# Transposes of the attention probabilities as two 64-row tiles, in turn with the scores by head

## Chip, cores, metric

The kernel runs on one core of one Trainium2 chip. The metric is the device time of one execution in microseconds (us). TensorE (PE) multiplies matrices into PSUM, VectorE (DVE) and ScalarE (ACT) read PSUM and SBUF, GpSimd (POOL) works in SBUF, and SyncE (SP) issues most of the DMA.

## The reference, cut to what matters

Attention with a bias that a small network makes of the relative positions, and behind it a gated feed-forward network (FFN) with a convolution over the sequence. There are 4 batches, 8 heads, 576 positions and 64 elements a head; all is float32.

```python
scores = scale * np.matmul(q, k.transpose(0, 1, 3, 2))      # (4, 8, 576, 576)
scores = scores + bias.transpose(2, 0, 1)[None, :, :, :]
scores = scores - np.max(scores, axis=-1, keepdims=True)
attn = np.exp(scores)
attn = attn / (np.sum(attn, axis=-1, keepdims=True) + 1e-09)
out = np.matmul(attn, v)
...
h = np.maximum(x @ w_in, 0.0)       # x: (4, 576, 512), w_in: (512, 1024)
...
return (h * gate @ w_out)
```

## The kernel before

The work has three stages: the bias (up to about 66 us, with the first units of attention between its steps), the attention loop (to about 316 us) and the FFN.

The attention loop goes over 16 passes `n` in `seq`, a pass being one pair of heads and one batch. A pass has five units `t` in the order 1, 2, 3, 4, 0 (`units`, line 85), and `ui` is a unit's place in that order. A unit of t = 1 to 4 is 128 query rows of both heads; the unit of t = 0 is the first 64 rows of both heads on top of each other, so it counts as one head (`heads`, line 544).

For each unit and head there are three steps. `scores` (line 327) multiplies q and k in two tiles of TensorE, 64 rows by 128 columns each, into two banks of a `psS` tile (two buffers); VectorE adds the bias and takes the row's minimum of the negative (line 348). `expo` (line 359) is one exponential on ScalarE, with the row's sum collected in `sms`. `transposes` (line 375) turns the probabilities, so that their keys lie on the partitions: four 128x128 blocks for each head on TensorE (line 388, as float32r against an identity), into one bank of `psT` (three buffers), which ScalarE copies to `pt` for head 0 and VectorE for head 1 (line 393). The last 64 keys of both heads are one further block (line 400) in a further bank, copied by VectorE (line 403). A small marker on ScalarE (line 323, `turned_sp`) precedes the transposes of head 0.

`pv_parts` (line 411) then multiplies v and `pt` in column tiles of 128 by 64. Its parts are kept in `fill` and are issued by `pv_share` after the transposes of the units at `ui` 0, 2 and 4. For most passes 20 instructions cover 256 or, for t = 0, 64 query columns. ScalarE copies the product out to `x` (lines 444 and 446).

The sums of a pass are inverted in the next one: `invert(n - 1)` on VectorE (lines 452 and 453), behind the unit at `ui` 1; a transpose of them by TensorE with the transposes of the unit at `ui` 2 (line 402), copied by VectorE (line 406); through DRAM by SyncE's DMA queue (`normalise`, line 461); and a multiplication on GpSimd (`apply_norm`, line 474), issued at `ui` 4.

The order of each engine's instructions is the order of the program. In the loop (line 604) an iteration `u` issues the scores of unit u + 2 and the exponentials of unit u + 1, head by head, then the transposes of unit u, head by head, each followed by one step of a weight job (`job_steps`: one step with ScalarE's line 96 and VectorE's line 97, then VectorE's lines 99 and 103, then GpSimd's lines 130 and 131), then `invert`, the products and the rest:

```python
for h in range(2):
    ...            # scores(*flat[u + 2], h); expo(*flat[u + 1], h)
for h in range(2):
    if h in heads(t):
        transposes(n, t, h, n - 1 if h and ui == 2 and n else None)
    next(job_steps, None)
```

Of the kernel before, what the change touches and what calls it, by code (L numbers as in the profile page):

```python
# [9 lines left out]
F32 = mybir.dt.float32  # L10
F32R = mybir.dt.float32r
# [8 lines left out]
def attention_ffn_kernel(  # L20
# [11 lines left out]
    nc = tc.nc  # L32
# [6 lines left out]
    P = 128  # L39
    TL = S % P  # L40
    NT = S // P
    NM = NT * P
# [23 lines left out]
    psT = pool(ctx, "psT", 3, space=PSUM)  # L66
# [8 lines left out]
    ident = const.tile([P, P], F32, name="ident")  # L75
    identr = const.tile([P, P], F32R, name="identr")
# [13 lines left out]
    def dve(o, i):  # L90
        nc.vector.tensor_copy(o, i)  # L91
# [41 lines left out]
    with tc.manual_schedule():  # L133
# [163 lines left out]
        r_p = pool(att, "r", 2)  # L297
        rb_p = pool(att, "rb", 1)

        rr_t = [vz_p.tile([P, P], F32, name=f"rr{i}") for i in range(2)]  # L300
        for r in rr_t:
            nc.gpsimd.memset(r, 0.0)
        rts = {}
# [71 lines left out]
        def transposes(n, t, h, sums=None):  # L375
            g = group(n, t)
            if (n, g) not in ptt:
                ptt[n, g] = pt_p.tile([P, 9, 2 * P], F32, name="pt") if g else pt0s[n % 2]
            pt = ptt[n, g]
            c0 = P if t == 2 or t == 4 and n else 0  # L380
            cs = slice(c0, c0 + P)
            if h == 0:
                turned_sp(n, t)
            spf = spt[n, t][0]
            ps = psT.tile([P, 512], F32, name="tp")
            for c in range(4):
                j = 5 * h + c
                tr = nc.tensor.transpose(  # L388
                    ps[:, c * P:(c + 1) * P].bitcast(F32R), spf[:, j * P:(j + 1) * P], identr
                )  # L390
                if c == 0:
                    tc.add_manual_dep(tr.ins, exps.pop((n, t, h)).ins.name, DATA)
            (dve if h else act)(pt[:, 5 * h:5 * h + 4, cs], ps.rearrange("p (c x) -> p c x", c=4))
            if h or not t:
                ps = psT.tile([P, 512], F32, name="tp")


                rows = P if t else TL
                cols = P if n else rows
                nc.tensor.transpose(ps[0:cols, 0:P].bitcast(F32R), spf[:, NM:NM + cols], identr)  # L400
                if sums is not None:
                    nc.tensor.transpose(ps[:, P:2 * P], rr_t[sums % 2], ident)
                dve(pt[0:rows, 4, cs], ps[0:rows, 0:P])
                if sums is not None:
                    rts[sums] = r_p.tile([9, P], F32, name="rt")
                    dve(rts[sums], ps[0:9, P:2 * P])

        ops_t = {}
        waiting = {}
# [1 line left out]
        def pv_parts(n, g):  # L411
            p, b = seq[n]
# [3 lines left out]
            def part(c):  # L416
# [7 lines left out]
                for h in range(2):  # L424
                    hs = slice(D * h, D * h + D)
                    if g:
                        slot = (0 if h else 5) if c == 4 else 6 + c if h else 1 + c
                        rhs = pt[:, 4 if c == 4 else 5 * h + c, 0:width]
                    else:
                        slot = 10 + c if h else 1 + c  # L430
                        rhs = pt[:, c, TL * h:TL * h + TL]
                    nc.tensor.matmul(  # L432
                        po[hs, oc], vt[:, slot, :], rhs, start=(c == 0), stop=(c == 4)
                    )
# [169 lines left out]
        for u, (n, t) in enumerate(flat):  # L604
            p, b = seq[n]
            ui = units.index(t)
            for h in range(2):
# [2 lines left out]
                        scores(*flat[u + 2], h)  # L610
                if u + 1 < NU and h in heads(flat[u + 1][1]):
                    expo(*flat[u + 1], h)
            for h in range(2):
                if h in heads(t):
                    transposes(n, t, h, n - 1 if h and ui == 2 and n else None)
                next(job_steps, None)
# [25 lines left out]
            if u + 2 < NU:  # L642
                n2, t2 = flat[u + 2]
                p2, b2 = seq[n2]
                if b2 == B - 1 and p2 + 1 < NP:
                    load_bias(p2 + 1, t2)
            if ui == 1 and n > 0:
                invert(n - 1)

            parts = len(fill) if u < 4 else pv_share[ui]  # L650
# [217 lines left out]
```

## Time and profile before

| | |
|---|---|
| median of 3 runs | 533.89 us (531.12 to 534.03) |
| profiled execution, its own time | 534.86 us |
| its span in the trace | 533.1 us |
| PE, DVE, ACT, POOL busy | 505.7, 385.4, 303.5, 103.9 us |

Busy time is the time covered by an engine's instructions in the record. PEld is the loading of weights into TensorE, which can lie under its matmuls. The end of a matmul is modelled and comes after its last column was streamed, so the distance between the starts of two matmuls tells the cost of the first, and a block's duration is longer than its share of the engine. A float32 multiplication of `scores` or `pv_parts` shows as two instructions.

### The profile page before, as it was taken

To read this page: it belongs to the slowest core of one execution; us is meant where nothing else is said; L and a number is where in the kernel's file an instruction comes from. 1 tells how busy PE (TensorE), PEld (TensorE's weight loads), DVE (VectorE), ACT (ScalarE), POOL (GpSimd) and SP (SyncE) were. 2 spreads that over 40 slices of the span, in tenths; PEclk is the share of its full clock that TensorE was granted. 3 is DMA by queue.
4 is the path that set the end of the run, shared out by engine and by line. 5 is a ranking of instruction groups with operands and counts; after the bars stand their busy time and mean duration, and the time that the engine had idled before them with its cause. 6 is when DMAs were issued, how large, how long until landed. Compare 5 with 4: busy or idle time off the path is not lost.

```text
span 533.1 us, 10413 instructions
## 1 busy us (share of the span) xinstructions
PE 505.7 (95%) x3871; PEld 376.4 (71%) x3871; DVE 385.4 (72%) x888; ACT 303.5 (57%) x733; POOL 103.9 (19%) x123
## 2 busy tenths in 40 slices
PE   5988999999999999999989999799999999999995
PEld 3332466676666666666656678788998899899984
DVE  6989685676778778788776854994699169928910
ACT  5888785677666777666775654652362135215510
POOL 1000000112222222212222521571016002500000
PEclk9999999999899999999998999989999999999998
DMA  6689654697556975579753121000100200020011
GB/s 158 251 242 354 220 136 109 152 292 181 153 140 157 299 185 155 139 177 289 190 138 86 60 80 46 0 2 6 73 1 0 81 20 1 1 79 2 1 39 59
DMA packets 32700, 63.40 MB, mean 119 GB/s; under 512 B 5490, under 2 KB 11146, under 8 KB 32650
## 3 DMA queue, kind: packets, MB, share of 16 engines
q1 hardware_dynamic: 32506, 62.66, 40.4%
q8 instruction: 30, 0.49, 0.4%
q14 instruction: 20, 0.16, 0.1%
q10 hardware_dynamic: 144, 0.08, 0.1%
HBM read 46.74 MB, written 15.98 MB: 118 GB/s over the span
## 4 chain that ended last, share of the span: by engine, by line
PE 59%; DMA 10%; DVE 8%; POOL 3%; issue 3%; ACT 2%; SPq 1%; POOLq 0%; DVEq 0%
PE s L495 17%; PE tp L719 14%; PE o L432 10%; PE s L341 8%; PE tp L388 5%; PE o L719 4%; DMA r_d<-rt 3%; DMA rb<-r_d 3%; DVE sp L348 2%; POOL x L474 2%; DMA qk<-in_qk_dram 1%; DMA vt<-in_v_dram 1%; DVE cv L694 1%; DVE pt L91 1%; ACT sp L362 1%
## 5 line engine op out<-in xcount | busy, mean ns | idle before, releaser
L348 DVE CUSTOM_DVE_ANT_0 sp<-s,bt 128x576 f32<-128x576 f32 x144 | 103.4, 750 | 52.2 <-PE s L341 35.8
L362 ACT ACTIVATE sp<-sp,nm 128x576 f32<-128x576 f32 x144 | 110.2, 769 | 8.9 <-DVE nm L348 8.9
L495 PE MATMUL s<-xs,wi 128*128 128x288 f32 x768 | 106.4, 301 | 2.9 <-ACT h L507 2.9
L495 PEld LDWEIGHTS s<-xs,wi 128*128 128x128 f32 x768 | 105.4, 193 | 3.4 <-ACT h L507 3.1
L341 PE MATMUL s<-qk 64*128 64x288 f32 x640 | 100.7, 431 | 2.2 <-DVE nm L348 1.9
L432 PE MATMUL o<-pt,vt 128*64 128x256 f32 (+2 forms) x940 | 89.8, 338 | 0.7 <-ACT x L88 0.7
L388 PEld LDWEIGHTS tp<-identr,sr 128*128 128x128 f32 x576 | 53.9, 140 | 34.8 <-issue 20.8
L341 PEld LDWEIGHTS s<-qk 64*128 64x128 f32 x640 | 54.7, 186 | 30.7 <-issue 7.1
L432 PEld LDWEIGHTS o<-pt,vt 128*64 128x64 f32 x940 | 53.9, 139 | 24.4 <-issue 2.2
L88 ACT ACTIVATE pt<-tp 128x512 f32<-128x512 f32 x80 | 46.9, 586 | 41.4 <-PE tp L388 41.4
L719 PE MATMUL tp<-wo,g 128*128 128x512 f32 x288 | 70.1, 389 | 0.0
L388 PE MATMUL tp<-identr,sr 128*128 128x128 f32 x576 | 66.2, 254 | 2.8 <-DVE pt L91 2.8
L91 DVE COPY pt<-tp 128x512 f32<-128x512 f32 (+2 forms) x144 | 60.8, 458 | 6.0 <-PE tp L400 3.1
L694 DVE SCALAR_TENSOR_TENSOR cv<-h,cw,cv 128x575 f32<-128x575 f32 x64 | 60.4, 944 | 2.4 <-ACT cv L689 0.4
L719 PEld LDWEIGHTS tp<-wo,g 128*128 128x128 f32 x288 | 54.0, 188 | 11.0
L474 POOL TENSOR_TENSOR x<-x,rb 128x576 f32<-128x576 f32 x16 | 23.3, 1453 | 177.4 <-ACT sr L323 90.6
L260 PE MATMUL s<-y,pars 128*32 128x512 f32 (+8 forms) x352 | 45.9, 502 | 5.0 <-ACT st L286 2.2
L243 DVE TENSOR_SCALAR y<-tl,inv,nb 128x512 f32<-128x512 f32 (+8 forms) x116 | 49.8, 504 | 0.0
L507 ACT ACTIVATE h<-s 128x576 f32<-128x576 f32 x32 | 20.8, 651 | 47.2 <-PE s L495 47.1
L700 ACT ACTIVATE cv<-cv 128x576 f32<-128x576 f32 x32 | 21.8, 682 | 29.7 <-DVE cv L694 29.7
L260 PEld LDWEIGHTS s<-y,pars 128*32 128x32 f32 x352 | 15.2, 113 | 29.3 <-DVE y L243 13.2
L130 POOL TENSOR_SCALAR xs<-x 128x576 fp32r<-128x576 f32 x16 | 15.1, 945 | 83.5 <-PE s L495 83.5
(68 smaller groups left out, 486.6 us busy)
## 6 DMA issues: line engine op xcount, KB each, us to landing
qk<-in_qk_dram SPq DMA_DIRECT2D x32, 320.0 KB
bt<-bias_d SPq DMA_DIRECT2D x32, 288.0 KB
bias_d<-st SPq DMA_DIRECT2D x14, 607.0 KB
qk<-in_qk_dram SPq DMA_DIRECT2D x32, 144.0 KB
rb<-r_d SPq DMA_DIRECT2D x32, 144.0 KB
out_dram<-o SPq DMA_DIRECT2D x17, 256.0 KB
raw_w<-in_moe_w_in_dram SPq DMA_DIRECT2D x16, 256.0 KB
vt<-in_v_dram SPq DMA_DIRECT2D x16, 224.0 KB
```

What stands on the lines that cost most here:

```text
L88: nc.scalar.activation(o, i, AF.Copy)
L91: nc.vector.tensor_copy(o, i)
L243: nc.vector.tensor_scalar(y, dist[:, 0:n], inv[:, ig:ig + 1], nb1, op0=ALU.mult, op1=ALU.max)
L260: nc.tensor.matmul(ps[32 * j:32 * j + 32, a // 512 if n > 512 else blk % 2, 0:min(n - a, 512)], w2b, ys[j][:, a:min(n, a + 512)], start=Tr ...
L341: nc.tensor.matmul(ps[:, a, 0:HS], qt[rows, qo:qo + P], qt[rows, KO + hh * HS:KO + hh * HS + HS], start=(i == 0), stop=(i == len(ops) - 1),)
L348: nc.vector.tensor_tensor_reduce(out=halves(spt[n, t][0][:, h]), in0=ps[:, :, 0:HS], in1=halves(bt[:, h]), op0=ALU.add, op1=ALU.min, scale ...
L362: exps[n, t, h] = nc.scalar.activation(sp[:, h], sp[:, h], AF.Exp, bias=nm[:, h:h + 1], scale=-1.0, accum_out=sms[n][:, col:col + 1],)
L388: tr = nc.tensor.transpose(ps[:, c * P:(c + 1) * P].bitcast(F32R), spf[:, j * P:(j + 1) * P], identr)
L432: nc.tensor.matmul(po[hs, oc], vt[:, slot, :], rhs, start=(c == 0), stop=(c == 4))
L495: nc.tensor.matmul(ps[:, a, 0:HS], wi[c][:, pw, cs], xss[b, c][:, px, a * HS:(a + 1) * HS], start=(i == 0), stop=(i == 3 * KC - 1),)
L694: nc.vector.scalar_tensor_tensor(out=cv[:, o:o + S - 1], in0=h[:, i:i + S - 1], scalar=cw[:, f, kk:kk + 1], in1=cv[:, o:o + S - 1], op0=AL ...
L719: nc.tensor.matmul(ps, lhs(f, gi), wo[f][:, wj, cs], start=(f == 0 and i == 0), stop=(f == FC - 1 and i == 2),)
```

## The change

Each transpose of 128 rows becomes two of 64 rows in the two row tiles that the scores use. The results of the two row halves go to two banks, `ps[0]` and `ps[1]`, so every call of `transposes` takes two `psT` tiles, where head 0 took one and head 1 two. The last block goes into the same banks, after the four blocks for t = 0 and ahead of them in the order of issue for head 1. ScalarE copies the first half and VectorE the second, for both heads: 256 columns each, or 320 with the last block; for t = 0 with its 64 rows the last block is a copy of its own. `pt` is laid out anew (blocks 0 to 3 head 0, 4 to 7 head 1, 8 the last). The transpose of the inverted sums becomes two of 64 rows, with two copies.

In the loop the two passes over the heads become one: scores, exponential and transposes of head 0, then those of head 1. `invert(n - 1)` moves from the unit at `ui` 1 to that at `ui` 0, from n = 2 on.

```diff
@@ transposes
-            ps = psT.tile([P, 512], F32, name="tp")
-            for c in range(4):
-                j = 5 * h + c
-                tr = nc.tensor.transpose(
-                    ps[:, c * P:(c + 1) * P].bitcast(F32R), spf[:, j * P:(j + 1) * P], identr
-                )
...
-            (dve if h else act)(pt[:, 5 * h:5 * h + 4, cs], ps.rearrange("p (c x) -> p c x", c=4))
-            if h or not t:
-                ps = psT.tile([P, 512], F32, name="tp")
...
-                nc.tensor.transpose(ps[0:cols, 0:P].bitcast(F32R), spf[:, NM:NM + cols], identr)
-                if sums is not None:
-                    nc.tensor.transpose(ps[:, P:2 * P], rr_t[sums % 2], ident)
-                dve(pt[0:rows, 4, cs], ps[0:rows, 0:P])
-                if sums is not None:
-                    rts[sums] = r_p.tile([9, P], F32, name="rt")
-                    dve(rts[sums], ps[0:9, P:2 * P])
+            last = h or not t
+            rows = P if t else TL
+            blocks = [(4 * h + c, (5 * h + c) * P, P) for c in range(4)]
+            if last:
+                blocks.insert(4 - 4 * h, (8 if t else 4, NM, P if n or t else TL))
+            ps = [psT.tile([P, 512], F32, name="tp").rearrange("p (c x) -> p c x", x=TL) for _ in range(2)]
+            halves_ = [slice(TL * a, TL * a + TL) for a in range(2)]
+            for k, (bk, j, cols) in enumerate(blocks):
+                for a, ra in enumerate(halves_):
+                    tr = nc.tensor.transpose(
+                        ps[a][0:cols, bk - 4 * h].bitcast(F32R), spf[ra, j:j + cols], identr[ra, ra]
+                    )
+                    if k == 0 and a == 0:
+                        tc.add_manual_dep(tr.ins, exps.pop((n, t, h)).ins.name, DATA)
+            if sums is not None:
+                for a, ra in enumerate(halves_):
+                    nc.tensor.transpose(ps[a][:, 5], rr_t[sums % 2][ra], ident[ra, ra])
+            for a, copy in ((0, act), (1, dve)):
+                cs = slice(c0 + TL * a, c0 + TL * a + TL)
+                if rows == P:
+                    copy(pt[:, 4 * h:4 * h + len(blocks), cs], ps[a][:, 0:len(blocks)])
+                else:
+                    copy(pt[:, 0:4, cs], ps[a][:, 0:4])
+                    copy(pt[0:rows, 4, cs], ps[a][0:rows, 4])
+            if sums is not None:
+                rts[sums] = r_p.tile([9, P], F32, name="rt")
+                for a, ra in enumerate(halves_):
+                    dve(rts[sums][:, ra], ps[a][0:9, 5])
@@ pv_parts
-                        rhs = pt[:, 4 if c == 4 else 5 * h + c, 0:width]
+                        rhs = pt[:, 8 if c == 4 else 4 * h + c, 0:width]
@@ the loop over u
                     expo(*flat[u + 1], h)
-            for h in range(2):
                 if h in heads(t):
                     transposes(n, t, h, n - 1 if h and ui == 2 and n else None)
                 next(job_steps, None)
...
-            if ui == 1 and n > 0:
+            if ui == (0 if n > 1 else 1) and n > 0:
                 invert(n - 1)
```

## Rows read from the trace of the kernel before

**Rows 1.** Busy time of each engine, with the number of instructions, the mean granted share of TensorE's clock, the share of the DMA engines and GB/s, in four stretches that begin and end at the transposes of a unit t = 0: thirteen passes, one quiet pass, and two long ones.

```profile
88.26:301.95 213.69, 207.47 (x1849) 140.36 (x1847) 161.67 (x475) 148.27 (x419) 54.16 (x73) 0.98 0.65 175
186.80:202.24 15.44, 15.44 (x145) 10.56 (x143) 12.40 (x38) 11.52 (x35) 3.98 (x6) 1.00 0.75 190
136.49:154.42 17.93, 17.33 (x145) 11.49 (x143) 12.55 (x39) 11.19 (x33) 4.49 (x7) 0.91 0.57 145
267.03:286.25 19.22, 17.48 (x145) 11.46 (x143) 12.55 (x39) 11.19 (x32) 4.48 (x7) 0.91 0.52 134
```

**Rows 2.** The timeline of TensorE's matmuls in the quiet pass: start, duration, line, operation, tiles, shape and count. L341 are scores, L388 and L400 transposes, L432 products with v.

```profile
187.35 2.38 PE L432 MATMUL o<-pt,vt 128*64 128x256 f32 x20
189.66 1.24 PE L341 MATMUL s<-qk 64*128 64x288 f32 x8
190.84 0.87 PE L388 MATMUL tp<-identr,sr 128*128 128x128 f32 x8
191.54 0.24 PE L400 MATMUL tp<-identr,sr 128*128 128x128 f32 x1
191.72 0.80 PE L432 MATMUL o<-pt,vt 128*64 128x64 f32 x20
192.45 1.24 PE L341 MATMUL s<-qk 64*128 64x288 f32 x8
...
194.33 0.25 PE L400 MATMUL tp<-identr,sr 128*128 128x128 f32 x1
194.50 1.24 PE L341 MATMUL s<-qk 64*128 64x288 f32 x8
```

**Rows 3.** The waits of TensorE over the whole span: who waited for whom, us in total, how often, and the longest.

```profile
PE tp L388 <- DVE pt L91: 2.8, 4, 1.5
...
PE tp L402 <- DVE rr L453: 1.9, 7, 0.4
...
PE s L341 <- DVE nm L348: 1.9, 5, 0.7
```

**Rows 4.** The timeline in narrow windows of 0.01 to 0.4 us around 107 us, each row with the instructions that reach into its window: transposes and their loads, then loads of scores (the first two, and the first four), then matmuls of scores (the first four, and the first six).

```profile
107.85 0.42 PE L388 MATMUL tp<-identr,sr 128*128 128x128 f32 x3
107.90 0.31 PEld L388 LDWEIGHTS tp<-identr,sr 128*128 128x128 f32 x3
...
106.56 0.19 PEld L341 LDWEIGHTS s<-qk 64*128 64x128 f32 x2 [0.38 <-issue]
...
106.56 0.30 PEld L341 LDWEIGHTS s<-qk 64*128 64x128 f32 x4 [0.38 <-issue]
...
106.56 0.76 PE L341 MATMUL s<-qk 64*128 64x288 f32 x4
...
106.56 1.00 PE L341 MATMUL s<-qk 64*128 64x288 f32 x6
```

**Rows 5.** The chain of work that ended last, in order of time, in the FFN: start, duration, line and count. L495 streams 288 columns an instruction, L719 512.

```profile
373.45 25.58 PE s L495 x192
399.03 2.06 PE tp L719 x9
```

**Rows 6.** Copies out of PSUM, grouped by line and shape: count, then busy time in us and mean ns of one, then the idle time of the engine just before them.

```profile
L88 ACT ACTIVATE pt<-tp 128x512 f32<-128x512 f32 x80 | 46.9, 586 | 41.4 <-PE tp L388 41.4
L91 DVE COPY pt<-tp 128x512 f32<-128x512 f32 x64 | 43.7, 683 | 2.8 <-PE tp L388 2.8
...
L91 DVE COPY pt<-tp 128x128 f32<-128x128 f32 x64 | 17.8, 279 | 0.0
...
L88 ACT ACTIVATE x<-o 128x64 f32<-128x64 f32 x15 | 3.3, 220 | 1.7 <-PE o L432 0.9
```

**Rows 7.** The timeline of ScalarE in the quiet pass: a copy of a product, two exponentials, the marker, a copy of transposes, a step of a weight job, a copy of 64 columns and the next exponential.

```profile
189.78 0.60 ACT L88 ACTIVATE x<-o 128x512 f32<-128x512 f32 x1 [1.45 <-PE o L432]
190.27 0.77 ACT L362 ACTIVATE sp<-sp,nm 128x576 f32<-128x576 f32 x1
...
191.03 0.77 ACT L362 ACTIVATE sp<-sp,nm 128x576 f32<-128x576 f32 x1
...
191.79 0.19 ACT L323 ACTIVATE sr<-pars 128x2 fp32r<-128x2 f32 x1
191.89 0.58 ACT L88 ACTIVATE pt<-tp 128x512 f32<-128x512 f32 x1
192.36 0.42 ACT L96 ACTIVATE u<-raw_w 128x256 f32<-128x256 f32 x1
192.69 0.21 ACT L88 ACTIVATE x<-o 128x64 f32<-128x64 f32 x1
192.79 0.77 ACT L362 ACTIVATE sp<-sp,nm 128x576 f32<-128x576 f32 x1
```

**Rows 8.** The timeline of TensorE, VectorE and ScalarE at the start of the first long stretch: four transposes of head 0, VectorE's copies of the unit before, ScalarE's copy of these four, and the transposes of head 1 that waited.

```profile
132.63 0.53 PE L388 MATMUL tp<-identr,sr 128*128 128x128 f32 x4
...
132.99 0.88 DVE L91 COPY pt<-tp 128x512 f32<-128x512 f32 x2
...
133.20 0.60 ACT L88 ACTIVATE pt<-tp 128x512 f32<-128x512 f32 x1 [0.61 <-PE tp L388]
...
133.73 0.53 PE L388 MATMUL tp<-identr,sr 128*128 128x128 f32 x4 [0.57 <-DVE pt L91]
```

More of the change, by code (lines that the diff above doesn't have):

```diff
@@ L380, in transposes @@
             c0 = P if t == 2 or t == 4 and n else 0
-            cs = slice(c0, c0 + P)
             if h == 0:
@@ L384, in transposes @@
             spf = spt[n, t][0]
-            ps = psT.tile([P, 512], F32, name="tp")
-            for c in range(4):
-                j = 5 * h + c
-                tr = nc.tensor.transpose(
-                    ps[:, c * P:(c + 1) * P].bitcast(F32R), spf[:, j * P:(j + 1) * P], identr
-                )
-                if c == 0:
-                    tc.add_manual_dep(tr.ins, exps.pop((n, t, h)).ins.name, DATA)
-            (dve if h else act)(pt[:, 5 * h:5 * h + 4, cs], ps.rearrange("p (c x) -> p c x", c=4))
@@ L394, in transposes @@
-            if h or not t:
-                ps = psT.tile([P, 512], F32, name="tp")
-                rows = P if t else TL
-                cols = P if n else rows
-                nc.tensor.transpose(ps[0:cols, 0:P].bitcast(F32R), spf[:, NM:NM + cols], identr)
-                if sums is not None:
-                    nc.tensor.transpose(ps[:, P:2 * P], rr_t[sums % 2], ident)
-                dve(pt[0:rows, 4, cs], ps[0:rows, 0:P])
-                if sums is not None:
-                    rts[sums] = r_p.tile([9, P], F32, name="rt")
-                    dve(rts[sums], ps[0:9, P:2 * P])
+            last = h or not t
```

## Prediction

> **What bounds the kernel now.** I read the attention loop pass by pass; a pass is the five units of one batch and head pair. The busy times by stretch [rows 1] show the reader two things. In a quiet pass (186.80 to 202.24 us) TensorE is busy for all 15.44 of 15.44 us, ScalarE for 11.52 and VectorE for 12.40: TensorE sets the pass. Over thirteen passes the mean is 213.69 / 13 = 16.44 us, so 1.00 us a pass is something else; two passes of 17.93 and 19.22 us, with a mean granted clock of 0.91, hold 6.27 us of it. The timeline of TensorE in the quiet pass [rows 2] shows the order that the change breaks up: a unit's scores (8 instructions), then its transposes (8 and 1), then in three of five units the products with v (20). The waits of TensorE [rows 3] show who causes the excess: VectorE, late with reciprocals, copies and minima.
>
> **The transposes.** Each 128-row transpose becomes two of 64 rows, 64 columns streamed instead of 128, in two tiles. Three matmuls of a block of transposes take 0.42 us, the last of which lasts 0.25 as in [rows 2], so they start 0.085 us apart; with the block's own ends in [rows 2] (190.84 to 191.54 for eight, first load included) 0.087. I use 0.087. The loads are not hidden: they start 0.05 us after the matmul [rows 4]. The slope between 288 and 512 streamed columns, (2.06/9 - 25.58/192) us over 224 columns, is 0.00043 us a column [rows 5], so 128 columns stream in 0.054 and the load takes the other 0.033. The trace has no transpose in a 64-row tile. Lowest bound: the stream alone, 0.027 us a pair. Highest: a load like that of the scores, which are in this mode. Their second pair of loads starts 0.30 - 0.19 = 0.11 us after the first [rows 4], so 0.11 + 0.027 = 0.137 a pair. Two tiles one after the other, 2 x 0.060 = 0.120, lie inside. The scores' two tiles do run together (a second pair, 0.24 us, is paid once for two instructions: 0.76 and 1.00 us for four and six [rows 4]), and the load in transposing took 0.033 at the same 128 columns. So I take 0.033 + 0.027 = 0.060 a pair. A pass has 4 x 9 + 5 = 41 blocks: 41 x (0.087 - 0.060) = 1.11 us less.
>
> The Trainium skill, "TensorE: Matmul & The Clock Gate", section "LDWEIGHTS (loading the stationary operand)", speaks against this: a load costs its columns, whatever its rows, about columns / 1.2 ns, which is an estimated 107 ns for 128, so halving the rows buys no load time. By that figure a pair would cost an estimated 0.134 us and the 41 blocks 1.9 us more, not 1.11 less. The trace agrees for the scores (0.11 us [rows 4]) and not for the transposes, whose load and stream together take 0.087.
>
> **Mode edges and order.** A unit's scores take 1.18 us up to the first transpose (189.66 to 190.84 [rows 2]), where a load of 0.11 and four pairs of 0.24 make 1.07: 0.11 lost at the edge, five times a pass. From the last transpose to scores (194.33 to 194.50) or to the products (191.54 to 191.72) is 0.17 to 0.18 against 0.054 of stream: 0.12 lost. In one mode the five edges and two of the 0.12 go (-0.79). But scores and transposes now alternate by head, so nine stretches of scores instead of five begin with an exposed load of 0.11: +0.44. (At best those loads hide and cost nothing; at worst the edges stay, +0.79.) Written out: 8 stretches of 0.11 + 2 x 0.24 = 0.59, one of 1.07 (t = 0, one head), 41 x 0.060 = 2.46, products 2.31 + 2.31 + 0.73, three edges 0.36, the sums' transposes 0.12: **14.08 us of TensorE a pass** against 15.44.
>
> **The copies.** ScalarE's copy of 512 columns takes 0.586 us and one of 64 takes 0.220 [rows 6], 0.00082 a column: 256 cost 0.38 and 320 cost 0.43. The cadence on ScalarE [rows 7] runs 0.11 below the durations (512 columns 0.47), so they occupy 0.27 and 0.32; an exponential occupies 0.76, the marker of line 323 0.10. ScalarE's unit is 2 x 0.76 + 0.10 + 0.27 + 0.32 = 2.21 us, before 2.09. VectorE's 0.683 and 0.279 [rows 6] become 0.42 and 0.48 by the same 0.00105 a column, 0.06 less a unit, given back in the unit of t = 0 (two copies for one) and in the second copy of the sums. Its load stays near 12.5 us a pass, under TensorE's.
>
> **The new wait.** psT has three buffers. A call of transposes took one or two tiles, three a unit, so each buffer had a whole unit to be emptied. Now every call takes two, and its second is the buffer that ScalarE empties for the call just before it. On ScalarE that copy stands behind an exponential of the next unit (and, for the first head, line 323); behind the waiting transpose on TensorE stand the next scores, and VectorE and then ScalarE wait for those. So calls cannot follow each other faster than ScalarE's half unit, 1.13 or 1.08 us, where TensorE needs 0.83 or 0.89. I write a pass out by hand: a copy starts 0.22 us after its call is through (132.63 + 4 x 0.087 to 133.20), and TensorE goes on 0.06 us after a copy of 0.68 that began at 132.99 (133.73) [rows 8]; x copies start 0.12 us after the scores behind the products do [rows 2, 7].
>
> Unit t = 1 starts at 0: x copy 0.12 to 0.61, exponential to 1.37, marker, copy of head 0 from 1.47, landed 1.85; head 1 would start at 1.42 and starts at 1.91: 0.49 lost. Unit 2 starts at 3.06 behind the products; x copy to 3.28, exponential, copy landed 4.52; head 1 wanted 4.48, starts 4.58: 0.10. Unit 3 has scores for one head alone, so its two calls are adjacent: head 1 wanted 6.19, copy landed 6.79, starts 6.85: 0.66. The products of 2.31 us let ScalarE catch up; unit 4 loses 0.07 and unit 0 0.12. Sum 1.44: **a pass takes 14.08 + 1.44 = 15.52 us**, where 15.44 was. The weight jobs' ScalarE step (0.33 us [rows 7], half of the units) falls into such halves about once: 15.85 in passes with jobs.
>
> **The reciprocals.** Two VectorE instructions move one unit up, past that unit's work, from the third pass on; no DMA moves with them, since the sums' way to DRAM still starts after the transposes of t = 3. They take away seven waits, 1.9 us in all, of line 402 [rows 3]. I count nothing for this: the same call now waits 0.66 us for ScalarE.
>
> **The sum.** Thirteen passes held eleven ordinary ones, 213.69 - 17.93 - 19.22 = 176.54 us. Mine: 4 x 15.52 + 7 x 15.85 = 173.0, 3.5 less, because the old waits for VectorE fall into the new ones. The two long passes and the FFN I leave as they are. The profiled execution took 534.86 us, 1.76 over its span, and the median of the runs is 0.2% under it: 534.86 - 3.5 = 531.4 and 533.89 - 3.5 = 530.4; I say 531.
>
> **The rivals.** (a) TensorE's gain comes through: the copies land before the call asks, or the pair is at its low bound. For: ScalarE has 3.9 us idle in a quiet pass [rows 1]. Against: its order puts an exponential before each copy. Whole gain: 15 passes x 1.36 = 20 us, 514; with the pair at 0.027 and the wait in place, the 20 to 25 blocks on the path save some 0.7 us a pass, 522.
> (b) Slower: the pair is dear. As a mechanism of this kernel: a load of 0.11 as in the scores, 0.137 a pair, makes TensorE 14.08 + 41 x 0.077 = 17.24 a pass; with half of the old excess 17.7 against 16.44, 15 passes, 19 us more, 553; at 0.120 (tiles in turn) 543. It decides from 14.08 + 41 x (p - 0.060) + 0.5 = 16.44, a pair of 0.105 us. Against: the 0.033 us load. The rule of the Trainium skill cited above ("TensorE: Matmul & The Clock Gate", on LDWEIGHTS) is the case for it.
> (c) The clock. The two passes at a mean of 0.91 hold stretches at 1.2 GHz instead of 2.4, after TensorE had stood idle. Now it idles 9% in short waits; if every second or third pass had such a stretch, at about 0.09 x 18 = 1.7 us each, five more cost 8 us: 540 after the 531.
>
> **How the numbers follow.** My forecast 0.41, (a) 0.31, (b) 0.20, (c) 0.08. Its own range is 526 to 538. What a measurement here can tell from no change is about 1%, 528.6 to 539.2. Faster: most of (a) and 0.07 of my case, 0.36. Slower: most of (b) and (c) and 0.02, 0.27. Same: 0.37. The range 517 to 545 leaves out the whole gain of (a) and the dear half of (b), under 0.2.
>
> **What would show it.** Right: pairs of transposes 0.06 us apart, no 0.11 edge between scores and transposes, and a new wait of TensorE at the transposes for ScalarE's copies (line 88), some 20 us in all, with quiet passes of 15.4 to 15.9 us. Wrong: no such wait and passes near 14.2 (a); pairs over 0.1 us (b); more clock rows under 2.4 GHz (c). No wait of the sums' transposes for the reciprocals should be left.

## The result, and the profile after

| | before | after |
|---|---|---|
| median of 17 runs each | 533.05 us (529.97 to 536.25) | 536.35 us (532.57 to 541.34) |
| ratio, 95% interval | | 1.006 (1.0035 to 1.0086) |
| profiled execution, its span | 534.86, 533.1 us | 535.10, 533.3 us |
| thirteen passes, from one profile | 213.69 us | 214.66 us |

The change made the kernel 0.6% slower; I had forecast 0.5% faster. A few executions, here the one of 541.34 us, and 600.25 and 670.18 us among the runs of e4 and e9 below, count as slow and stay out of every ratio. The two profiled executions differ by 0.24 us only, since that of before lies 1.8 us over its median and that of after 1.25 us under its own. So the traces show some 1 us of the 3.3 us in the attention loop (and 0.8 us the other way behind it: 231.15 and 230.38 us); the rest lies in executions that no trace shows.

The busy times by stretch of the changed kernel answer to [rows 1]: thirteen passes, a quiet pass, and the longest of the thirteen (columns as there).

```profile
88.26:302.92 214.66, 201.68 (x2393) 146.46 (x2393) 161.82 (x501) 155.18 (x485) 54.05 (x73) 0.99 0.67 176
171.43:187.46 16.03, 15.32 (x186) 11.20 (x185) 12.45 (x41) 12.04 (x40) 3.67 (x5) 1.00 0.86 255
136.33:155.54 19.21, 16.79 (x186) 11.75 (x184) 12.40 (x41) 12.13 (x39) 3.63 (x5) 0.91 0.57 139
```

TensorE's busy time in the loop fell from 207.47 to 201.68 us, yet the loop is longer. In a quiet pass TensorE is no longer busy throughout: 15.32 of 16.03 us. Going by the starts of the products, quiet passes now take 15.8 to 16.05 us, where before had 15.44.

TensorE's waits over the whole span, with VectorE's behind its weight jobs, answer to [rows 3]:

```profile
PE tp L397 <- ACT pt L88: 7.6, 26, 0.5
PE tp L397 <- DVE pt L91: 5.0, 4, 2.2
```

```profile
DVE w L97 <- POOL wi L131: 8.0, 4, 2.5
```

The wait for ScalarE's copies is there, 26 times; the wait of the sums' transposes for the reciprocals is gone; the wait for VectorE's copies has grown from 2.8 to 5.0 us, its longest from 1.5 to 2.2, and 1.2 us more are waited for its copies of the sums. VectorE waits another 4.6 us for L131 on `wo`, 12.6 us in all; before it was 6.6 for `wi` and 4.2 for `wo`. (A wait is counted from the modelled end of the last matmul, so the gap between the starts is some 0.2 us longer.)

The timeline of TensorE in the quiet pass answers to [rows 2]:

```profile
174.12 0.65 PE L397 MATMUL tp<-identr,sr 64*128 64x64 f32 x8
174.59 0.76 PE L341 MATMUL s<-qk 64*128 64x288 f32 x4
174.96 0.40 PE L397 MATMUL tp<-identr,sr 64*128 64x64 f32 x1
175.63 0.58 PE L397 MATMUL tp<-identr,sr 64*128 64x64 f32 x9 [0.26 <-ACT pt L88]
...
176.87 0.76 PE L341 MATMUL s<-qk 64*128 64x288 f32 x4
177.25 0.64 PE L397 MATMUL tp<-identr,sr 64*128 64x64 f32 x8
177.72 0.75 PE L341 MATMUL s<-qk 64*128 64x288 f32 x4
...
179.79 0.67 PE L397 MATMUL tp<-identr,sr 64*128 64x64 f32 x8
180.91 0.58 PE L397 MATMUL tp<-identr,sr 64*128 64x64 f32 x9 [0.45 <-ACT pt L88]
```

Where nothing waits, one head's scores and four pairs of transposes take 0.85 us (176.87 to 177.72). The two places that lose most are those that the prediction named: the second head of the first unit (one transpose at 174.96, the other nine not before 175.63) and the two calls of the unit t = 3 (179.79 and 180.91, though four pairs alone would be through by 180.12). These are adjacent, since the scores issued there are those of t = 0, for one head alone.

What a pair costs is read from one block of transposes in narrow windows, each of which cuts the same block a little later, so that the row holds what has started by then:

```profile
186.36 0.25 PE L397 MATMUL tp<-identr,sr 64*128 64x64 f32 x2
...
186.36 0.34 PE L397 MATMUL tp<-identr,sr 64*128 64x64 f32 x4
...
186.36 0.51 PE L397 MATMUL tp<-identr,sr 64*128 64x64 f32 x8
```

The instructions come in twos, so the two tiles do run side by side. But each further pair adds (0.51 - 0.25) / 3 = 0.087 us, or 0.083 by the whole row of nine (four steps in 0.58 - 0.25 us, as at 175.63). I use 0.083; a whole block of 128 rows took 0.087 before.

The copies, grouped by line and shape, answer to [rows 6]:

```profile
L88 ACT ACTIVATE pt<-tp 128x256 f32<-128x256 f32 x80 | 30.0, 375 | 31.1 <-PE tp L397 31.0
...
L88 ACT ACTIVATE pt<-tp 128x320 f32<-128x320 f32 x64 | 27.7, 432 | 7.8 <-PE tp L397 7.0 <-PE tp L404 0.8
...
L91 DVE COPY pt<-tp 128x256 f32<-128x256 f32 x80 | 33.5, 419 | 6.2 <-PE tp L397 6.2
L91 DVE COPY pt<-tp 128x320 f32<-128x320 f32 x64 | 31.0, 485 | 1.1 <-PE tp L397 0.6 <-PE tp L404 0.4
```

They cost what was worked out: 0.38, 0.43, 0.42 and 0.48 us.

The longest pass shows where its time goes. These are lines of the timeline of all engines around its stall, and the busy times of two stretches of it:

```profile
139.59 1.13 SPq L477 DMA_DIRECT2D rb<-r_d  x2
...
143.32 1.41 POOL L483 TENSOR_TENSOR x<-x,rb 128x576 f32<-128x576 f32 x1 [7.11 <-ACT pt L88]
...
145.18 0.72 POOL L131 TENSOR_TENSOR wi<-w,wi 128x256 fp32r<-128x256 f32 x1
...
145.93 0.29 DVE L97 TENSOR_SCALAR w<-raw_w 128x256 int32<-128x256 int32 x1 [2.15 <-POOL wi L131]
...
146.82 0.48 DVE L91 COPY pt<-tp 128x320 f32<-128x320 f32 x1
...
147.36 0.59 PE L397 MATMUL tp<-identr,sr 64*128 64x64 f32 x10 [2.15 <-DVE pt L91]
...
147.98 3.88 PE L441 MATMUL o<-pt,vt 128*64 128x256 f32 x20
```

```profile
145.20:147.36 2.16, 0.01 (x2) 0.01 (x2) 1.43 (x5) 0.98 (x5) 0.70 (x1) 1.00 0.11 34
...
148.70:152.10 3.40, 3.40 (x18) 1.73 (x16) 0.93 (x4) 0.67 (x3) 1.13 (x2) 0.50 1.01 254
```

Read it from the top: SyncE issues the transfer of the reciprocals at 139.59. GpSimd stood 7.11 us before its multiplication by them (`apply_norm`), so its weight step (L131) ended at 145.90. The row puts the wait down to a copy by ScalarE, but that is only what came last by the record: wherever GpSimd waits in the sixteen passes, the multiplication starts 3.6 to 4.6 us after the transfer's issue, here 3.73, and thirteen of the sixteen waits are put down to the transfer. So I read it as the transfer. VectorE's next weight step (L97) waits for GpSimd's, and VectorE's bias step and copy out of psT stand behind it. The transposes wait for the copy: TensorE does next to nothing for 2.16 us. Soon after, the granted clock is 0.50, 1.2 GHz, for 3.40 us, and the twenty instructions of the products take 3.88 us instead of 2.38 [rows 2].

The same chain stands ahead of the stall in the kernel before, at 133.73 [rows 8], with a stretch of 3.40 us at a granted clock of 0.50 from 136.5 us on. GpSimd's multiplication and VectorE's weight step there:

```profile
130.15 1.42 POOL L474 TENSOR_TENSOR x<-x,rb 128x576 f32<-128x576 f32 x1 [7.27 <-DMA rb<-r_d]
...
132.78 0.29 DVE L97 TENSOR_SCALAR w<-raw_w 128x256 int32<-128x256 int32 x1 [3.42 <-POOL wi L131]
```

### The profile page after: what moved, and what is told of

Read it like the earlier page. It is cut to its first block, busy times and chain, and to the rows that moved or that the text cites. A ratio compares the mean times of both kernels' runs of the same rounds, so it can differ in the third digit from the quotient of the medians.

```text
span 533.3 us, 11854 instructions
## 1 busy us (share of the span) xinstructions
PE 498.9 (94%) x4542; PEld 382.3 (72%) x4542; DVE 386.1 (72%) x919; ACT 311.6 (58%) x813; POOL 103.3 (19%) x123
## 3 DMA queue, kind: packets, MB, share of 16 engines
HBM read 46.74 MB, written 15.98 MB: 118 GB/s over the span
## 4 chain that ended last, share of the span: by engine, by line
PE 57%; DMA 11%; ACT 7%; DVE 6%; POOL 2%; issue 2%; SPq 1%; POOLq 0%; DVEq 0%; ACTq 0%
PE s L504 17%; PE tp L727 14%; PE o L441 10%; PE s L341 7%; PE tp L397 5%; PE o L727 4%; ACT sp L362 3%; DMA qk<-in_qk_dram 3%; DMA r_d<-rt 3%; DMA rb<-r_d 3%; DMA bt<-bias_d 2%; ACT pt L88 2%; POOL x L483 1%; DVE cv L702 1%; DVE sp L348 1%
## 5 line engine op out<-in xcount | busy, mean ns | idle before, releaser
L348 DVE CUSTOM_DVE_ANT_0 sp<-s,bt 128x576 f32<-128x576 f32 x144 | 107.8, 750 | 50.6 <-PE s L341 41.2
L397 PE MATMUL tp<-identr,sr 64*128 64x64 f32 x1312 | 110.7, 265 | 14.0 <-ACT pt L88 7.6
L341 PE MATMUL s<-qk 64*128 64x288 f32 x640 | 119.3, 449 | 1.2 <-DVE nm L348 1.1
L397 PEld LDWEIGHTS tp<-identr,sr 64*128 64x128 f32 x1312 | 78.3, 136 | 42.3 <-ACT pt L88 20.4
L504 PE MATMUL s<-xs,wi 128*128 128x288 f32 x768 | 105.2, 299 | 2.7 <-ACT h L516 2.7
L504 PEld LDWEIGHTS s<-xs,wi 128*128 128x128 f32 x768 | 104.1, 191 | 3.4 <-ACT h L516 2.9
L441 PE MATMUL o<-pt,vt 128*64 128x256 f32 (+2 forms) x940 | 88.6, 336 | 0.7 <-ACT x L88 0.7
L88 ACT ACTIVATE pt<-tp 128x256 f32<-128x256 f32 (+2 forms) x160 | 59.3, 381 | 39.0 <-PE tp L397 38.0
L91 DVE COPY pt<-tp 128x256 f32<-128x256 f32 (+2 forms) x160 | 66.5, 424 | 7.3 <-PE tp L397 6.8
L341 PEld LDWEIGHTS s<-qk 64*128 64x128 f32 x640 | 54.1, 185 | 19.6 <-issue 6.1
```

Source lines behind the costliest of these rows:

```text
L88: nc.scalar.activation(o, i, AF.Copy)
L341: nc.tensor.matmul(ps[:, a, 0:HS], qt[rows, qo:qo + P], qt[rows, KO + hh * HS:KO + hh * HS + HS], start=(i == 0), stop=(i == len(ops) - 1),)
L348: nc.vector.tensor_tensor_reduce(out=halves(spt[n, t][0][:, h]), in0=ps[:, :, 0:HS], in1=halves(bt[:, h]), op0=ALU.add, op1=ALU.min, scale ...
L397: tr = nc.tensor.transpose(ps[a][0:cols, bk - 4 * h].bitcast(F32R), spf[ra, j:j + cols], identr[ra, ra])
L441: nc.tensor.matmul(po[hs, oc], vt[:, slot, :], rhs, start=(c == 0), stop=(c == 4))
L504: nc.tensor.matmul(ps[:, a, 0:HS], wi[c][:, pw, cs], xss[b, c][:, px, a * HS:(a + 1) * HS], start=(i == 0), stop=(i == 3 * KC - 1),)
```

## The experiments

All ratios are to the kernel before, with their 95% intervals. "Loop" is the stretch of thirteen passes, from the products of one pass to the same products thirteen passes later, in the run's profile (213.69 us for the kernel before by these marks too); where its row is shown, it has the stretch, its us, then busy time of PE, PEld, DVE, ACT and POOL, granted clock, DMA share and GB/s. "After" and "before" behind a label say which kernel was edited.

### What the row tiles bring: e1, e7

**e1_full_blocks** (after): transposes of 128 rows again, in the changed kernel's order and with its two copies. Blocks 0 and 1 go to the bank that ScalarE empties, the others to VectorE's.

```diff
-            for k, (bk, j, cols) in enumerate(blocks):
-                for a, ra in enumerate(halves_):
...
+                a, s = min(k // 2, 1), k if k < 2 else k - 2
+                tr = nc.tensor.transpose(ps[a][0:cols, s * P:s * P + P].bitcast(F32R), spf[:, j:j + cols], identr)
...
+            act(pt[:, 4 * h:4 * h + 2, cs], v3[0][:, 0:2])
```

> The changed kernel with its order by head, its two psT tiles a call and its copy for each of ScalarE and VectorE, but with transposes of 128 rows again (blocks 0 and 1 in one bank, the others in the second). Theory P (a pair of 64-row transposes costs as much as one 128-row transpose, 0.083 against 0.087 us, so the tile form saves only the mode edges): the edges come back at nine places instead of five, some 9 x (0.11 + 0.12) = 2.1 us a pass less the loads that were exposed anyway, partly hidden under the wait for ScalarE; 545 to 560 us. Rival T (the tile form itself costs time and the order is harmless): 530 us or less.

Measured: 544.01 us, 1.0181 (1.0136 to 1.0226). The loop:

```profile
89.56:311.35 221.79, 219.37 (x1849) 136.71 (x1847) 169.15 (x489) 153.29 (x471) 54.07 (x73) 1.00 0.64 170
```

The time lies 1 us under the range of Theory P. So against blocks of 128 rows in the same order the tile form is worth (221.79 - 214.66) / 13 = 0.55 us a pass. The stalls of the changed kernel are in that number, and e1, at a granted clock of 1.00, has few: its quiet passes take 16.95 us, so that between quiet passes the tile form is worth about 1.0 us. (The copies of the calls with the last block aren't divided alike: 256 and 384 columns here, twice 320 there.) Against the old order, with its fewer edges, that isn't enough: e3 below has the price of the order.

**e7_tile_after_tile** (after): all transposes of a call's first tile, then all of the second.

```diff
-            for k, (bk, j, cols) in enumerate(blocks):
-                for a, ra in enumerate(halves_):
+            for a, ra in enumerate(halves_):
+                for k, (bk, j, cols) in enumerate(blocks):
```

> The changed kernel with a call's transposes issued tile after tile (all of the first 64 rows, then all of the second) and not in turn. A pair cost 0.083 us where 0.060 was forecast. Theory S (in a 64-row tile a load takes 0.056 us, and the two tiles work side by side): a single transpose then costs 0.083, a pair 0.166, 41 x 0.083 = 3.4 us more a pass, partly under the waits, 560 to 590 us. Rival Q (the two tiles' loads take turns, 0.028 us each): a single one costs 0.055, a pair 0.11, 1.1 us more a pass, 540 to 553 us. Rival R (loads of one tile hide under the other's stream only when tiles alternate; a single tile is as in 128 rows): in between.

Measured: 538.6 us, 1.0114 (1.0055 to 1.0173), loop 215.50 us. A call of eight, cut by narrow windows as above:

```profile
183.49 0.47 PE L397 MATMUL tp<-identr,sr 64*128 64x64 f32 x3
...
183.49 0.55 PE L397 MATMUL tp<-identr,sr 64*128 64x64 f32 x5
...
183.49 0.64 PE L397 MATMUL tp<-identr,sr 64*128 64x64 f32 x7
```

The transposes still start in twos, 0.08 to 0.09 us apart, though the program has those of one tile behind each other: the tiles' sequences run side by side also when they are issued one after the other. The theory that they would then run one after the other is refuted, and with it the time that it gave. This alone leaves rival Q open, that the two tiles' loads take turns. But where the second tile has to wait, it works alone afterwards, here with its first two and then the last four of its five transposes, again in narrow windows:

```profile
291.69 0.33 PE L397 MATMUL tp<-identr,sr 64*128 64x64 f32 x2
...
291.78 0.50 PE L397 MATMUL tp<-identr,sr 64*128 64x64 f32 x4
```

The second starts 0.09 us after the first, and the four take three steps of (0.50 - 0.25) / 3 = 0.083 us. So 0.083 us is what one transpose of 64 rows costs in a tile that works alone, where rival Q had 0.055: it is no cost of alternating between tiles, and none of sharing the loads.

### What the order by head costs: e3, e10

**e3_merge_only** (before): the loop by head and the early reciprocals, with the old transposes of 128 rows.

```diff
                     expo(*flat[u + 1], h)
-            for h in range(2):
                 if h in heads(t):
...
-            if ui == 1 and n > 0:
+            if ui == (0 if n > 1 else 1) and n > 0:
```

> The kernel before with the order by head and the earlier reciprocals, but its own transposes and copies. Theory P: mode edges at nine places instead of five and no new wait for ScalarE (three psT tiles a unit): 4 more edges both ways and loads, 4 x 0.34 = 1.4 us a pass, 548 to 556 us. Rival T: the order is harmless, 530 to 535 us.

Measured: 538.79 us, 1.0103 (1.0068 to 1.0137). The loop, and TensorE's timeline over two heads:

```profile
90.09:306.47 216.38, 216.26 (x1848) 135.84 (x1846) 162.66 (x475) 151.71 (x419) 54.00 (x73) 1.00 0.65 174
```

```profile
185.50 0.76 PE L341 MATMUL s<-qk 64*128 64x288 f32 x4
186.19 0.53 PE L388 MATMUL tp<-identr,sr 128*128 128x128 f32 x4
186.65 0.76 PE L341 MATMUL s<-qk 64*128 64x288 f32 x4
```

TensorE is busy for 216.26 of 216.38 us, and almost every pass takes 16.61 us. Scores of one head and four transposes take 1.15 us here and 0.85 us in the changed kernel: this 0.30 us, at equal prices of a block and a pair, is what going over to the other mode and back costs a head, with whatever load lies open there. The order by head costs the old transposes 16.61 - 15.44 = 1.17 us a pass, which is four more such ways there and back, 4 x 0.30; the tile form saves the edges that this order has multiplied. The time misses both expected ranges, for the loop is only 2.7 us longer than before: at 16.61 us a pass the excess of 1.00 us over the quiet pass is gone.

**e10_tiles_old_loop** (after): the new transposes with the old loop, scores of both heads ahead of the transposes of both.

```diff
                     expo(*flat[u + 1], h)
+            for h in range(2):
                 if h in heads(t):
```

> The changed kernel with the loop order of before: scores and exponentials of both heads, then the transposes of both. The two calls of a unit then stand next to each other, and the second needs the buffer that ScalarE has just begun to copy. Theory W: each unit waits for a copy (0.38 us and what stands ahead of it on ScalarE) less what the exposed loads cost; 540 to 552 us. Rival: the order by head only adds exposed loads, and without it the tiles save them; 530 us or less.

Measured: 575.86 us, 1.0782 (1.0733 to 1.083). The loop, and the wait of TensorE that makes it:

```profile
91.96:339.11 247.15, 206.70 (x2394) 157.53 (x2393) 168.00 (x501) 157.50 (x484) 54.54 (x74) 0.95 0.58 153
```

```profile
PE tp L397 <- ACT pt L88: 47.1, 62, 1.1
```

Two calls in a row need four psT tiles, and there are three. The wait is up to 1.1 us, and passes take 18.2 us at the least, so the time lies far above both expected ranges: with three psT tiles and without the order by head the new transposes are a loss of 7.8%.

### The wait for ScalarE: e2, e8, e9

**e2_copy_first** (after): the transposes of a head, and so ScalarE's copy, go ahead of the next unit's exponential.

```diff
-                if u + 1 < NU and h in heads(flat[u + 1][1]):
-                    expo(*flat[u + 1], h)
                 if h in heads(t):
                     transposes(n, t, h, n - 1 if h and ui == 2 and n else None)
+                if u + 1 < NU and h in heads(flat[u + 1][1]):
+                    expo(*flat[u + 1], h)
```

> The changed kernel with the transposes of a head issued ahead of the exponential of the next unit, so that ScalarE copies a call's results before that exponential and not behind it. Theory W (TensorE waits 1.2 to 1.5 us a pass for ScalarE's copies, which stand behind an exponential): most of the 22 us of load idle for ScalarE's copies goes, 1 us a pass, 518 to 526 us. Rival T (the pair's own cost sets the time): no change, 534 to 538 us. Rival E (the exponentials become late in their turn): slower than 537 us, with waits of the transposes or of ScalarE for minima.

Measured: 540.27 us, 1.0126 (1.0083 to 1.017), loop 218.72 us. TensorE's waits, then VectorE's:

```profile
PE tp L397 <- DVE pt L91: 9.6, 10, 2.9
...
PE tp L397 <- ACT pt L88: 3.7, 14, 0.4
```

```profile
DVE w L97 <- POOL wi L131: 10.9, 4, 3.2
```

The wait for ScalarE is halved, as it should be, and the shortest passes fall to 15.5 us. But the wait for VectorE doubles, three passes take 17.8 to 20.0 us, and Theory W's 518 to 526 us are missed.

**e8_short_exp** (after) and **e9_before_short_exp** (before): each exponential covers 64 of the 576 keys and leaves out the other 512, so that ScalarE is through early.

```diff
-                sp[:, h], sp[:, h], AF.Exp, bias=nm[:, h:h + 1], scale=-1.0,
+                sp[:, h, 0:64], sp[:, h, 0:64], AF.Exp, bias=nm[:, h:h + 1], scale=-1.0,
```

> The changed kernel with exponentials of 64 of the 576 keys, the other keys left as they are: ScalarE's half unit falls from 1.1 to about 0.7 us and no longer sets the pace. Theory W (the wait for ScalarE's copies costs 1.2 us a pass): quiet passes of 14.6 to 15.0 us, 517 to 523 us. Rival D (VectorE and the transfers then set the same pace): 530 us or more.

> The kernel before with exponentials of 64 of the 576 keys, the other keys left as they are. ScalarE sets nothing there, so quiet passes stay at 15.44 us; 528 to 534 us by theory W. If it gains as much as the changed kernel does, ScalarE's pace was no property of the change.

Measured: 538.25 us, 1.0076 (1.0038 to 1.0113) with the changed kernel, loop 217.95; 532.27 us, 0.9981 (0.9941 to 1.0021) with the kernel before, loop 211.91. The changed kernel's loop and waits with the short exponentials (e8):

```profile
87.52:305.47 217.95, 206.12 (x2393) 148.50 (x2392) 159.26 (x503) 111.69 (x484) 53.72 (x73) 0.96 0.66 173
```

```profile
PE tp L397 <- DVE pt L91: 8.9, 9, 3.7
...
PE tp L397 <- ACT pt L88: 1.7, 5, 0.4
```

The outcome is that of e2, with ScalarE's load cut by 43 us: its wait is gone but for 1.7 us, quiet passes take 15.4 to 15.5 us, and the time is no better than the changed kernel's, because two passes of 20.4 and 21.4 us hold stalls for VectorE of up to 3.7 us and the mean granted clock falls to 0.96. So the wait for ScalarE isn't what keeps the kernel from being faster by itself. The nearer TensorE comes to what stands behind it, the more it meets VectorE held up by GpSimd: VectorE's waits behind L131 on `wi`, 8.0 us in the changed kernel, are 11.5 us here.

### The reciprocals: e4, e5

**e4_late_invert** (after): the reciprocals at their old place. **e5_early_invert_only** (before): they alone move. The line is the second edit in e3's diff: e4 takes it back, and e5 has nothing else.

> The changed kernel with the reciprocals at their old place. Theory W (the sums' transposes would wait for ScalarE in any case): 536 to 539 us, waits of the sums' transposes for the reciprocals of 1 to 3 us in all. Rival: the earlier reciprocals are worth what they removed and more, 540 us or above.

> The kernel before with the reciprocals one unit sooner and nothing else. If the waits of the sums' transposes for the reciprocals (3 us of load idle in the loop) are real cost there, 529 to 532 us. Rival: VectorE is late there anyway and the same time is waited for its copies; no change, 532 to 535 us.

Measured: e4 536.81 us, 1.0056 (1.002 to 1.0092), loop 213.91, against 536.35 and 214.66 with them early; e5 532.62 us, 0.9992 (0.9959 to 1.0025). By itself the move brings nothing that is measured, in either kernel. (The profiled execution of e5 was its fastest, 529.46 us, and its loop of 210.18 us stands for no more than that.)

### GpSimd's multiplication: e11 to e15

If GpSimd's wait for the reciprocals' way through DRAM is behind the stalls, then a multiplication that is issued later, behind weight steps that it used to hold up, ends the stalls. **e11_late_norm** (after) issues it in the next pass:

```diff
-            if ui == 4 and n > 0:
+            if ui == 1 and n > 1:
+                apply_norm(n - 2, rb)
+            if ui == 4 and n == NSEQ - 1:
                 apply_norm(n - 1, rb)
```

**e12_before_late_norm** has the same edit in the kernel before, with the early reciprocals; **e13_copy_first_late_norm** in e2.

> The changed kernel with GpSimd's multiplication by the reciprocals issued two units into the next pass and not at the end of its own, so that it no longer stands waiting for its DMA ahead of the weight jobs' GpSimd steps. Theory G (TensorE's long waits for VectorE's copies, 5 us in all and up to 2.2 at once, come from VectorE's line 97 standing behind that multiplication): the long passes of 17 to 19 us and the low clock behind them go; 526 to 531 us. Rival V (VectorE is late by its own load): no change, 534 to 538 us.

> The kernel before with the same later multiplication and the reciprocals one unit sooner. Theory G: the long passes go here too, most of the 1.0 us a pass above the quiet 15.44 us; 519 to 526 us. Rival V: 531 to 534 us.

> The changed kernel with the transposes ahead of the exponentials, as tried above, and the later multiplication. Theory G with W: its quiet passes were 15.5 us, its slowness lay in long passes (VectorE's line 97 behind GpSimd, 10.9 us); 522 to 528 us. Rival V: 538 us or more.

Measured: e11 529.65 us, 0.9934 (0.9903 to 0.9965); e12 522.49 us, 0.9806 (0.9767 to 0.9846); e13 526.96 us, 0.988 (0.9839 to 0.9921). Their loops, and the waits of TensorE in e11:

```profile
88.35:296.06 207.71, 199.25 (x2394) 145.92 (x2393) 164.68 (x501) 154.91 (x485) 55.01 (x75) 1.00 0.69 181
```

```profile
88.31:291.12 202.81, 201.94 (x1847) 138.28 (x1846) 163.97 (x475) 147.75 (x420) 54.57 (x74) 1.00 0.70 186
```

```profile
88.31:294.10 205.79, 198.80 (x2394) 145.04 (x2393) 163.68 (x503) 158.84 (x484) 54.83 (x75) 1.00 0.70 183
```

```profile
PE tp L397 <- ACT pt L88: 8.2, 28, 0.5
...
PE tp L397 <- DVE pt L91: 1.7, 2, 0.9
```

In all three the granted clock of the loop is 1.00 and no pass is over 16.31 us, where after had 19.21. The wait for VectorE's copies falls from 5.0 to 1.7 us; that for ScalarE stays. GpSimd in e11, at the place of the stall shown above:

```profile
141.21 0.73 POOL L131 TENSOR_TENSOR wi<-w,wi 128x256 fp32r<-128x256 f32 x1
143.06 1.41 POOL L483 TENSOR_TENSOR x<-x,rb 128x576 f32<-128x576 f32 x1 [1.12 <-ACT pt L88]
```

The multiplication starts at about the same time as there (143.06 and 143.32), again 3.7 us after its transfer's issue (139.37). But the weight step is now ahead of it and ends at 141.94 instead of 145.90, and no wait of VectorE's line 97 for GpSimd's weight steps is left, where the changed kernel had six. e12 is 1.9% faster than the kernel before. And with the stalls gone the change itself can be read cleanly: e11 and e12 differ by the transposes, their copies and the order alone, 207.71 against 202.81 us, so **the change costs 4.9 us in thirteen passes, 0.38 us a pass**.

**e14_short_exp_late_norm** (after, e11 with e8) and **e15_before_norm_alone** (before, e12 with the reciprocals at their old place) take these two apart.

> The changed kernel with the later multiplication and exponentials of 64 of the 576 keys, the other keys left as they are: neither GpSimd nor ScalarE holds TensorE up, so a pass is TensorE's own work. Theory P (a pair of transposes costs what a block of 128 rows did, so the tile form and the order by head cancel): passes of 15.3 to 15.5 us as in the kernel before with the later multiplication (15.44), 521 to 525 us. By the forecast's 14.08 us it would be 503 to 508 us.

> The kernel before with the later multiplication alone, the reciprocals at their old place. Theory G: the long passes were GpSimd's, so it is within 3 us of the version that has both, 522 to 526 us. Rival: the reciprocals were worth more once the long passes were gone, 527 us or more.

Measured: e14 524.29 us, 0.9845 (0.9779 to 0.9912), loop 201.65, passes of 15.4 to 15.6 us (one of 16.3). e15 524.29 us, 0.9843 (0.98 to 0.9886), loop 204.53. One call of e14 in the timeline of TensorE, where it still waits:

```profile
219.72 0.65 PE L397 MATMUL tp<-identr,sr 64*128 64x64 f32 x8
220.61 0.80 PE L397 MATMUL tp<-identr,sr 64*128 64x64 f32 x10 [0.24 <-DVE pt L91]
```

Against e11 the exponentials' share of the wait is (207.71 - 201.65) / 13 = 0.47 us a pass. Even with that gone the changed kernel is only level with e12 (201.65 and 202.81 us), so its TensorE has no 1.36 us a pass to give. (The profiled execution of e14 was the fastest of four, 521.36 us; by the medians it is 1.8 us slower than e12.) The early reciprocals may be worth 1.8 us once the stalls are gone (524.29 against 522.49), but the intervals of e12 and e15 overlap: that stays open.

## Why the prediction was wrong

**The step that failed is the pair of transposes, "So I take 0.033 + 0.027 = 0.060 a pair".** It costs 0.083 us, as much as the block of 0.087 that it replaces, so the saving of 1.11 us a pass is next to nothing, 41 x 0.004 = 0.16. So the halved stream bought nothing. If it still costs 0.027, the load in a tile of 64 rows costs some 0.056 us, not the 0.033 of the old blocks; no run shows how the 0.083 divides. I chose by the row that was alike in operation (a transpose's load) instead of the one that was alike in mode (the scores' load, 0.11); the pair lies between the two prices, 0.060 and 0.137.

The Trainium skill, "TensorE: Matmul & The Clock Gate", section "LDWEIGHTS (loading the stationary operand)", has rows cost nothing and columns everything. The traces agree that half the rows don't make a load shorter: the loads' records, which overlap, last 0.140 us on the mean before and 0.136 us after. With its figure, an estimated 107 ns for 128 columns, the trace doesn't agree, since here the whole pair took 83 ns.

**Mode edges and order: right, to some 0.07 us a head.** The terms that don't hang on the pair stand up. One head's scores and four pairs were to take 0.59 + 4 x 0.083 = 0.92 with the measured pair, and took 0.85; e3 shows an edge of 0.30 us a head that the tile mode saves. TensorE's own pass is 14.08 + 41 x 0.023 = 15.02 us by the prediction's list; a pass of e14 (15.4 to 15.5 us) less the gap of some 0.35 us at its adjacent calls (four pairs from 219.93, when the scores of 1.07 us from 218.86 are through, to 220.26; the next call at 220.61) leaves about 15.1.

**The copies: right**, to 0.01 us.

**The new wait: right in its cause and its two main places, too large in sum.** I had 1.44 us a pass, and 0.33 more in the passes with weight jobs: on the mean (4 x 15.52 + 7 x 15.85) / 11 = 15.73 us a pass, 1.65 of it wait. In e11 it is 15.98 - 15.02 = 0.96. (I had said some 20 us in all; the view of after has 7.6 in 26 waits, some 13 with the 0.2 us that each wait lacks.) The two errors hang together, by an estimate: a call that takes 0.09 to 0.12 us longer at each of five waiting places leaves that much less to wait, some 0.5 us of the 0.7. So the dearer pairs are paid for in part by the wait: 0.94 more, 0.69 less, and a quiet pass of 15.98 us where I had 15.73. Over thirteen passes that is +3.2 us.

**The old waits.** I let the excess of the ordinary passes "fall into the new ones" and left the two long passes. Measured against e12 and e11, where the cause is taken away, the excess was 213.69 - 202.81 = 10.9 us before and is 214.66 - 207.71 = 6.95 us after; my sum amounts to 37.15 - 2 x 15.73 = 5.7 in it. So this was nearly right, 1.3 us short. That the excess comes from GpSimd is shown by e11 to e13 and e15; the prediction named VectorE alone, which stands behind GpSimd. The two parts, +3.2 and +1.3, are all that lies between my loop of 173.0 + 37.15 = 210.2 us and the 214.66 measured; they add up by the way they are taken, so the sum is no further proof.

**Luck.** The median of 536.35 us lies inside my range of 526 to 538, and 1% from the 531 that I gave, although the pair cost 38% more than I took: the shorter waits gave most of it back. The sign of the change was wrong all the same.

**The reciprocals: right**, counted as nothing (e4, e5), and their wait is gone.

**The rivals.** (a) fell: even e14, with ScalarE's wait mostly gone, has passes of 15.4 us, not 14.2. (b) didn't come with its price, but its turning point was wrong. I had put it at 0.105 us, from 14.08 + 41 x (p - 0.060) + 0.5 = 16.44, and so left the new wait out of the very case in which it stays. With it, 15.02 + 0.96 + 0.53 of excess = 16.51 us, what was measured, against 16.44: the turning point lies at a pair of some 0.081 us, a little under the price of the old block, and the pair landed on it. (c) didn't come in the profiled execution: the granted clock of the loop is 0.99 (0.98 before). But e8 shows that it can, with 0.96 and no gain from a faster ScalarE.

**What stays open** is the rest of the medians' difference, 3.3 us less the 0.24 of the profiled pair. In e11 and e12, without the stalls, the medians differ by 7.2 us and the loops by 4.9, and the profiles have 1.9 more behind the thirteen passes (231.2 and 229.4 us), which I didn't follow; how often a stall is followed by a stretch at the lower clock in executions without a profile was not measured.

## What to carry to other kernels

Cost an operation in a new tile mode by a row in that mode as well as by a row of the same operation, and work out the turning point of each rival with the waits that the forecast itself adds. Where an engine that feeds the bound keeps its program order, follow what stands ahead of its instructions, across engines: here a multiplication on GpSimd, waiting for a transfer, held up VectorE's copies and in the end TensorE, and moving it into the next pass was worth 1.6% by itself (e15). Before trying a change on a stage with such stalls, take them away first: the change's own cost, 4.9 us, could be read only then.

## What the runs showed of the hardware

- A transpose of 64 rows in a row tile takes 0.083 us, almost as long as one of 128 rows in the full array (0.087), also where its tile works alone (e7). Two tiles run side by side, whether their transposes are issued in turn (after) or tile after tile (e7).
- Passing from the scores' tiles to the full array and back costs 0.30 us for a head's scores and transposes (e3, 1.15 us, against after, 0.85).
- In the longest pass TensorE's idle 2.16 us was followed by 3.40 us at 1.2 GHz, granted clock 0.50. With GpSimd's multiplication issued in the next pass, behind weight steps that it used to hold up, the thirteen passes had 1.00 (e11 to e15).
- Slower passes can be without the stalls: e3, with passes of 16.61 us, kept the granted clock at 1.00 with GpSimd's multiplication at its old place, and TensorE was busy for all but 0.12 us of the thirteen passes. Which part of its edit did that wasn't taken apart.
